# Keys turned on VectorE from the fourth batch on, queries turned eight slots sooner, and zeroing moved, in pooled attention followed by a mixture of experts

## The chip, the cores and the metric

The kernel runs on one core of a Trainium2 chip. The core has TensorE (PE, matrix products into PSUM), VectorE (DVE), ScalarE (ACT), GpSimd (POOL, which here issues the loads) and SyncE (SP, which issues the first loads and all output stores). The metric is the time on the device of one execution, in microseconds (us); lower is better. The kernel before takes 555.17 us, the median of three runs (555.05 to 555.86).

## The reference

The inputs are `q`, `k`, `v` of shape 8 batches x 8 heads x 576 tokens x 64, and the weights of four experts. Keys and values are averaged over groups of 8 tokens, which leaves 72 of each, every query attends to these 72, and the result goes through all four experts, weighted by given probabilities:

```python
k_p = k.reshape(B, H, Sp, pool, D).mean(axis=3)      # Sp = 72, pool = 8
v_p = v.reshape(B, H, Sp, pool, D).mean(axis=3)
scores = scale * np.matmul(q, k_p.transpose(0, 1, 3, 2))
scores = scores - np.max(scores, axis=-1, keepdims=True)
attn = np.exp(scores)
attn = attn / (np.sum(attn, axis=-1, keepdims=True) + 1e-09)
return np.matmul(attn, v_p)
...
# x: 4608 tokens x 512 (all heads of a token side by side)
for e in range(E):                                   # 4 experts, 512 -> 1024 -> 512
    h = np.maximum(x @ w1[e], 0.0)
    out += p[:, e:e + 1] * (h @ w2[e])
```

## The kernel before, in words

The 4608 tokens are 36 tiles of 128 tokens (t = 0 to 35); four tiles are a group, for which the experts are run with 512 columns. A step is one expert on one group, so there are 36 steps. Each step has 12 slots: in slots 0 and 1 of every three the up projection of the next step is issued, one block of 128 hidden units per slot (`up`, L655, eight matmuls of 512 columns; ScalarE then applies the ReLU, L659), in the third the down projection of one tile of this step (`down`, L687, eight matmuls of 512 columns), which VectorE weights and adds up (`collect`, L698 and L702). The sums leave through SP. The up and down projections fill TensorE; attention for later tiles is fitted between them.

What is fitted where is written out by hand. `at(slot, function, arguments)` puts a call into a dictionary, and after the projection of a slot the calls of that slot are issued, in the order in which they were put there. Every engine works through its own instructions in the order of issue, so a slot fixes a place in each engine's queue and not a time; from slot 12 on a slot takes some 1.2 us of TensorE. Nothing is planned by a cost model.

`plan_tile(t, base, steps)` places attention for one tile. For tiles from DT = 9 on, `base` is 17 slots (tile 9: 14) before the slot in which the tile is due, thus 12 t - 65:

- `turn_q` (L454) at base: VectorE transposes the queries in blocks of 32 x 32 out of `qblk`, a buffer with one batch's queries (two buffers, loaded by `load_qblk`, L173, eight loads per batch of rows of 32 numbers). The result `qT` has four buffers.
- `scores` (L475) and `less_max` (L491, L498) at base + 2: TensorE multiplies `qT` by the turned keys `kT`, VectorE subtracts the row maximum.
- `expo` (L517, ScalarE) at base + 4; `normalise` (L541 to L544, VectorE) at base + 5: the row sums, their inverse, and the weights.
- `turn_e_part` (L571) at base + 6 to base + 9: VectorE turns the weights, 16 transposes of 32 partitions.
- `context_turned` (L629, TensorE, and L643, ScalarE) at base + 13: the products with the values.

Earlier tiles (t below 9) have their queries and weights turned by TensorE.

`plan_batch` places the work for one batch's keys and values, relative to the base of the first tile that needs that batch (from batch 3 on: tiles 13, 18, 22, 27 and 31, the batch edges). For keys: `fold_k` (L315) at base - 11 and base - 9 adds halves of the 8 pooled tokens, `end_k` (L325) at base - 8 does the last addition into `kpad`, `turn_k` at base - 5 turns it: five transposes on TensorE into PSUM (L344, `kT_ps`) and two copies by ScalarE (L353) into `kTh`, whose two halves (`y`) hold alternating heads with zeros between them. At end + 1, POOL loads the keys of the batch after next into the buffer that has become free (`load_k`, L107: `kraw`, two buffers). The values follow: folds at base - 1 and base, the last addition at base + 1 (L376), their spreading over blocks (L392) at base + 3, and the load of the batch after next at base + 2. The next batch's queries are loaded at base + 1, which waits until the buffer's last reader, `turn_q` of this tile, is done.

The prelude computes tiles 0 to 3 while expert weights arrive; it ends when the first weights of the second expert have landed. ScalarE zeroes several buffers at its beginning, and further ones after it: `vraw` (L903), then the mask `mask_h` (L286) in slot 1 and `kTh`, `eTh` and `vh` (L924) in slots 2 to 7. In the new kernel, KB = 3 is the first batch whose keys go the other way, WB = 2 is the one from which the halves `kTh` and `vh` are used, and BLK = 32, NW = 9, POOL = 8.

Of the kernel before, what the change touches and what calls it, by code (L numbers as in the profile page):

```python
# [12 lines left out]
BF16 = mybir.dt.bfloat16  # L13
# [4 lines left out]
def kernel(  # L18
# [10 lines left out]
    nc = tc.nc  # L29

    B, H, S, D = q.shape
    E, DM, F = moe_w1.shape
    P = nc.NUM_PARTITIONS
    POOL = 8
# [11 lines left out]
    NB = 5  # L46
    TAIL = ROWS - (NB - 1) * P
    DT = 2 * TPG + 1
    EXP_SCALE = 1.0 / (float(D) ** 0.5 * POOL)
    NZ = 4  # L50
    BLK = 32
# [3 lines left out]
    HR = ROWS // 2  # L55
    NW = HR // BLK

    SPAN = ((0, 0), (1, 0), (1, 1), (2, 1))
    assert H * D == DM and D == 64 and SP == 72 and P == 128 and TAIL == 64

# [4 lines left out]
    prep = ctx.enter_context(tc.tile_pool(name="prep", bufs=2))  # L65
# [15 lines left out]
    kraw = [raw.tile([P, NB, POOL * D], BF16, name=f"kraw{i}") for i in range(2)]  # L81
    vraw = [raw.tile([P, NB + 1, POOL * D], BF16, name=f"vraw{i}") for i in range(2)]
    ehalf, eTh, kTh = [], [], []
    vh = [raw.tile([P, len(SPAN), 2, 2, D], BF16, name=f"vh{i}") for i in range(2)]
    ebuf = [raw.tile([P, NB * P], BF16, name=f"ebuf{i}") for i in range(2)]
# [11 lines left out]
    def rows_of(src):  # L97
        return src.rearrange("h (j r) d -> (h j) (r d)", r=POOL)

    def load_rows(eng, dst, rows, parts=((0, NB - 1), (NB - 1, NB))):  # L100
        for i0, i1 in parts:
            if i1 == NB:
                src, to = rows[i0 * P:ROWS], dst[0:TAIL, i0, :]
            else:
                src = rows[i0 * P:i1 * P].rearrange("(i p) x -> p i x", p=P)
                to = dst[:, i0:i1, :]
            eng.dma_start(out=to, in_=src)  # L107

    def load_k(b):
        load_rows(nc.gpsimd, kraw[b % 2], rows_of(k[b]))  # L110

    def load_v(b):
        if b < WB:
# [85 lines left out]
    for c0 in range(0, TPG, 2):  # L199
        nc.sync.dma_start(  # L200
            out=qg[:, :, c0:c0 + 2, :],
            in_=q[0][:, 0:G, :].rearrange("h (p c) d -> p h c d", c=TPG)[
                :, :, c0:c0 + 2, :
            ],
# [16 lines left out]
    for sign, base in ((1, PW), (-1, -SP - 1)):  # L221
        nc.gpsimd.affine_select(
            out=own[:], in_=own[:], compare_op=ALU.is_ge, fill=0.0,
            base=base, channel_multiplier=sign,
# [5 lines left out]
    for sign, base in ((1, 0), (-1, SP - 1)):  # L230
        nc.gpsimd.affine_select(
            out=ownh[:], in_=ownh[:], compare_op=ALU.is_ge, fill=0.0,
            base=base, channel_multiplier=sign,
# [12 lines left out]
    load_w1(1)  # L246
    halves = (slice(0, FB // 2), slice(FB // 2, FB))
    load_k(1)
    load_q(TPG)
    load_w1(2, (0,))  # L250
# [25 lines left out]
    mask_v = const.tile([P, NB, MZ, D], BF16, name="mask_v")  # L276
    mask_h = const.tile([P, len(SPAN), 2, D], BF16, name="mask_h")

    def spread_mask():
        nc.scalar.copy(  # L280
            out=mask_v[:], in_=own[:, :, 1:NZ].unsqueeze(3).to_broadcast([P, NB, MZ, D])
        )

    def spread_mask_h():
        for n, (c, g) in enumerate(SPAN):
            nc.scalar.copy(  # L286
                out=mask_h[:, n], in_=ownh[:, c, g].unsqueeze(2).to_broadcast([P, 2, D])
            )
# [21 lines left out]
    kT, vblk, pads = {}, {}, {}  # L310

    def fold(rows, i0, i1, *widths):
        for n in widths:
            w = n * D
            nc.vector.tensor_add(  # L315
                out=rows[:, i0:i1, 0:w], in0=rows[:, i0:i1, 0:w],
                in1=rows[:, i0:i1, w:2 * w],
            )

    def last_k(b, rows, i0, i1, n=P):  # L320

        if b not in pads:
            pads[b] = prep.tile([P, NB, 2, D], BF16, name="kpad")
        shape = [n, i1 - i0, 2, D]
        nc.vector.tensor_add(  # L325
            out=pads[b][0:n, i0:i1],
            in0=rows[0:n, i0:i1, 0:D].unsqueeze(2).to_broadcast(shape),
            in1=rows[0:n, i0:i1, D:2 * D].unsqueeze(2).to_broadcast(shape),
        )

    def fold_k(b, n):
        fold(kraw[b % 2], 0, NB, n)

    def end_k(b):
        last_k(b, kraw[b % 2], 0, NB)

    def turn_k(b, odd=None, order=range(NB), between={}):

# [47 lines left out]
    def spread_v(b):  # L386
        if b >= WB:
            vblk[b] = vh[b % 2]
            for n, (c, g) in enumerate(SPAN):

# [231 lines left out]
    def context_turned(t):  # L622
        ps = ps_t.tile([P, KC, P], F32, tag="t", name="xT_ps")
        for b, _, n, at in segments(t * P, P):
            if t >= DT:
                for pair in range(NPAIR):
                    g, y = divmod(pair, 2)
                    for m in (2 * g, 2 * g + 1):
                        nc.tensor.matmul(  # L629
                            ps[:, pair, at:at + n],  # L630
                            lhsT=vblk[b][:, m, y].rearrange("p z d -> p (z d)"),
                            rhs=eT[t][:, SPAN[m][0], at:at + n, y],
                            start=(m == 2 * g), stop=(m == 2 * g + 1),
# [99 lines left out]
    SLOTS = 12  # L733
    plan = {}

    def at(slot, fn, *args):
        plan.setdefault(slot, []).append((fn, args))

    def plan_batch(b, fold4, fold2, end, turn, v_fold4, v_fold2, v_end, spread):
        at(fold4, fold_k, b, 4)  # L740
        at(fold2, fold_k, b, 2)
        at(end, end_k, b)
        at(turn, turn_k, b)
        if WB <= b < WB + 2:
            at(v_fold4 - 8, clear_v, b)
        at(v_fold4, fold_v, b, 4)
        at(v_fold2, fold_v, b, 2)
        at(v_end, end_v, b)
        at(spread, spread_v, b)
        if b + 2 < B:  # L750
            at(end + 1, load_k, b + 2)
            at(v_end + 1, load_v, b + 2)

    def plan_tile(t, base, steps):
        at(base, turn_q, t)
        at(base + steps[0], scores, t)
        at(base + steps[0], less_max, t)
        at(base + steps[1], expo, t)
        at(base + steps[2], normalise, t)
        if t < DT:  # L760
            at(base + steps[3], turn_e, t)
        else:
            for a in range(P // BLK):
                at(base + steps[3] + a, turn_e_part, t, a)
        at(base + steps[4], context_turned, t)
        return base + steps[4] + 1

    at(SLOTS - 4, domain_probs, dp1, TPG, DT)
    at(5 * SLOTS + 6, load_probs)
    at(7 * SLOTS + 5, domain_probs, dpr, DT, NT)  # L770
    plan_batch(1, 3, 4, 5, 7, 18, 19, 20, 21)
    for t in range(TPG, 2 * TPG):
        assert plan_tile(t, 12 + 3 * (t - TPG), (3, 5, 6, 9, 11)) <= 3 * SLOTS - 2
# [3 lines left out]
    for t in range(2 * TPG, NT):  # L777
        due = (t - TPG) * SLOTS
        if t < DT:
            lead, steps = 14, (2, 4, 5, 8, 10)  # L780
        else:

            lead, steps = 14 if t == DT else 17, (2, 4, 5, 6, 13)
        base = due - lead
        b = ((t + 1) * P - 1) // S
        if b > last_b:
            times = (-11, -9, -8, -5, -1, 0, 1, 3)
            if t == DT:
                times = (-6, -5, -4, -2, 2, 3, 4, 5)
            plan_batch(b, *(base + x for x in times))  # L790
            if 2 < b < B - 1:
                at(base + 1, load_qblk, b + 1)
            last_b = b
        assert plan_tile(t, base, steps) <= due - (0 if t == DT else 3)
# [3 lines left out]
    def warm(n):  # L798

        ps = ps_o.tile([P, 2 * P], F32, tag="o", name="warm_ps")  # L800
        for _ in range(n):
            nc.tensor.matmul(ps[:], lhsT=zero[:, 0:P], rhs=zero[:])

    act, dve = nc.scalar.copy, nc.vector.tensor_copy
    spread_mask()
    warm(22)
    fold(k0[0:TAIL], NB - 1, NB, 4, 2)
    last_k(0, k0, NB - 1, NB, TAIL)
# [81 lines left out]
    for i in range(2):  # L890
        for to, n, form in (
# [4 lines left out]
            part = room[:, at0:at0 + n]  # L896
            to.append(part.rearrange(form.pop("pattern"), **form))
            at0 += n
    zeros = [x for i in range(2) for x in (
        kTh[i][:], eTh[i][:, 2], vh[i][:, 1::2, :, 0]  # L900
    )]
    for t in vraw:
        nc.scalar.memzero(t[:, NB, :])  # L903
    at(1, spread_mask_h)
    for i, x in enumerate(zeros):
        at(2 + i, nc.scalar.memzero, x)
    load_k(2)
    load_qblk(2)
    load_v(2)
    load_qblk(3)  # L910

    for s in range(NSTEP):
        for slot in range(SLOTS):
            part, i = slot % 3, slot // 3
# [41 lines left out]
```

## Time and profile before

| | |
|---|---|
| median of three runs | 555.17 us (555.05 to 555.86) |
| the profiled execution | 555.2 us |
| its span, first to last instruction | 553.5 us |
| mean clock granted to TensorE | 0.999 of full speed |
| busy: TensorE, VectorE, ScalarE, POOL | 544.3, 384.9, 240.7, 81.7 us |
| up and down projections on TensorE (L655, L687) | 270.4 and 269.6 us |
| TensorE's waits that the profile lists | 5.4 us, 3.2 of them before the end of the prelude at 37.24 us |
| key transposes L344 on TensorE | 40, of 219 ns each, overlapping |

A line of the profile names the engine, the line of the kernel, the operation, the output and the inputs, the shapes and how many there are. In the order of time a line begins with its start and its length in us; what stands in brackets is the idle time of the engine ahead of it and what ended it. Matmuls overlap, so their lengths add up to more than the time that passes. Idle time of an engine that is not on the path that sets the end costs nothing.

### The profile page before, as it was taken

What the parts mean: (1) busy time and instruction counts of PE and PEld (TensorE: products, weight loads), DVE (VectorE), ACT (ScalarE), POOL (GpSimd) and SP (SyncE); (2) the same over time, 40 slices, a digit from 0 to 9 for tenths busy, and PEclk for the clock granted to TensorE, in tenths of its full rate; (3) what the DMA queues carried; (4) which work ended last, traced back from release to release, by engine and by line L of the source; (5) the groups of instructions that cost most, each with busy time, mean ns of one, the idle gap of its engine ahead of it and who ended that gap; (6) DMA issues with size and microseconds to landing.
All of it is one profiled execution on the core that took longest, in us unless ns stands there. A gap on an engine that the chain in (4) does not pass through costs nothing.

```text
span 553.5 us, 8005 instructions
## 1 busy us (share of the span) xinstructions
PE 544.3 (98%) x3110; PEld 270.6 (49%) x3110; DVE 384.9 (70%) x925; ACT 240.7 (43%) x422; POOL 81.7 (15%) x122
## 2 busy tenths in 40 slices
PE   7999999899999999999999999999999999999997
PEld 5854545444444444444444444444444444444444
DVE  5636946878977779877897778977897777622223
ACT  6764654344444444444444434444443444433330
POOL 6253381100240005100060004000000000000000
PEclk9999999999999999999999999999999999999999
DMA  9999999210590009900491019001000100001002
GB/s 226 207 200 206 182 110 197 43 6 0 101 103 2 1 38 108 60 1 19 101 60 27 2 76 44 1 1 58 19 2 0 53 25 1 2 38 39 0 1 76
DMA packets 88038, 33.69 MB, mean 61 GB/s; under 512 B 62656, under 2 KB 82944, under 8 KB 88000
## 3 DMA queue, kind: packets, MB, share of 16 engines
q0 software_dynamic: 75920, 21.44, 44.0%
q1 hardware_dynamic: 12080, 11.74, 6.3%
q8 instruction: 24, 0.39, 0.3%
q14 instruction: 14, 0.11, 0.1%
HBM read 45.16 MB, written 9.44 MB: 99 GB/s over the span
## 4 chain that ended last, share of the span: by engine, by line
PE 89%; DMA 5%; DVE 3%; POOL 1%; issue 0%; SPq 0%; DVEq 0%
PE o_ps L687 42%; PE h_ps L655 42%; DMA w<-in_moe_w_dram 5%; PE xT_ps L629 2%; PE sc L475 2%; DMA k<-in_k_dram 1%; DVE late L571 1%; POOL w L182 0%; DVE total L541 0%; PE kT_ps L344 0%; PE xT_ps L638 0%; PE last_ps L720 0%; DVE d_sb L498 0%; DVE ebuf L551 0%; DVE acc L698 0%
## 5 line engine op out<-in xcount | busy, mean ns | idle before, releaser
L655 PE MATMUL h_ps<-xT,w 128*128 128x512 bf16 x1120 | 270.4, 379 | 0.4 <-DMA w<-in_moe_w_dram 0.3
L687 PE MATMUL o_ps<-w,h_sb 128*128 128x512 bf16 x1144 | 269.6, 379 | 0.0
L659 ACT ACTIVATE h_sb<-h_ps 128x512 bf16<-128x512 f32 x280 | 167.1, 597 | 222.3 <-PE h_ps L655 221.6
L687 PEld LDWEIGHTS <-h_sb 128*128 128x128 bf16 x1144 | 111.9, 98 | 134.2
L655 PEld LDWEIGHTS <-w 128*128 128x128 bf16 x1120 | 106.3, 98 | 115.5 <-issue 1.0
L702 DVE SCALAR_TENSOR_TENSOR acc<-o_ps,p_sb,acc 128x512 f32<-128x512 f32 x107 | 80.2, 749 | 94.9 <-PE o_ps L687 93.6
L571 DVE STREAM_TRANSPOSE late<-late 32x64 f32<-32x64 f32 (+1 forms) x432 | 105.6, 244 | 6.9
L698 DVE TENSOR_SCALAR acc<-o_ps,p_sb 128x512 f32<-128x512 f32 x36 | 26.9, 747 | 34.9 <-PE o_ps L687 34.5
L173 POOL DMA_DIRECT2D qblk<-in_q_dram x48 | 38.9, 820 | 79.6 <-DVE qT L454 65.8
L643 ACT CAST xT<-xT_ps 128x512 bf16<-128x512 f32 x32 | 18.8, 586 | 49.5 <-PE xT_ps L629 42.9
L491 DVE TENSOR_REDUCE mx<-sc 128x8 f32<-128x576 f32 x34 | 25.7, 756 | 14.8 <-PE sc L475 14.4
L107 POOL DMA_DIRECT2D kraw<-in_k_dram x14 | 9.3, 667 | 146.6 <-DVE kpad L325 140.9
L498 DVE TENSOR_TENSOR d_sb<-sc,mx 128x576 f32<-128x576 f32 x34 | 25.7, 757 | 1.2
L541 DVE TENSOR_REDUCE total<-e_sb 128x8 f32<-128x576 f32 x32 | 23.8, 745 | 1.2 <-ACT e_sb L517 0.9
L544 DVE TENSOR_TENSOR late<-e_sb,rs 128x576 bf16<-128x576 f32 x27 | 21.7, 805 | 1.0
L517 ACT ACTIVATE e_sb<-d_sb 128x576 f32<-128x576 f32 x27 | 18.4, 683 | 5.0 <-DVE d_sb L498 4.7
L454 DVE STREAM_TRANSPOSE qT<-qblk 128x512 bf16<-128x512 bf16 (+1 forms) x30 | 19.1, 646 | 0.0
L629 PEld LDWEIGHTS <-vh 128*128 128x128 bf16 x240 | 14.8, 96 | 6.4
L475 PEld LDWEIGHTS <-qT 128*128 128x128 bf16 (+1 forms) x160 | 11.3, 100 | 11.4 <-DVE qT L454 2.8
L629 PE MATMUL xT_ps<-late,vh 128*128 128x128 bf16 (+1 forms) x240 | 16.8, 213 | 0.0
L124 POOL DMA_DIRECT2D vraw<-in_v_dram x24 | 14.5, 619 | 13.4 <-DVE v_half L376 12.4
L475 PE MATMUL sc<-late,qT 128*128 128x144 bf16 (+1 forms) x120 | 11.6, 227 | 1.8 <-DVE qT L454 1.8
(94 smaller groups left out, 201.8 us busy)
## 6 DMA issues: line engine op xcount, KB each, us to landing
out_dram<-acc SPq DMA_DIRECT2D x35, 256.0 KB, 2.0
w<-in_moe_w_dram POOLq DMA_DIRECT2D x12, 512.0 KB, 13.8
kraw<-in_k_dram POOLq DMA_DIRECT2D x7, 512.0 KB, 7.1
qblk<-in_q_dram POOLq DMA_DIRECT2D x48, 72.0 KB, 4.8
w<-in_moe_w_dram POOLq DMA_DIRECT2D x2, 1024.0 KB, 18.0
vraw<-in_v_dram POOLq DMA_DIRECT2D x6, 256.0 KB, 5.6
vraw<-in_v_dram POOLq DMA_DIRECT2D x6, 224.0 KB, 5.6
k<-in_k_dram SPq DMA_DIRECT2D x2, 512.0 KB, 4.5
```

Source lines behind the costliest of these rows:

```text
L173: nc.gpsimd.dma_start(out=to[:, g], in_=q[b][head:head + 2, :, half * BLK:(half + 1) * BLK] .rearrange("z (a i) d -> i (z a) d", i=BLK),)
L475: nc.tensor.matmul(banks[pair // 2][at:at + n, (pair % 2) * PW:(pair % 2 + 1) * PW], lhsT=qT[t][:, pair, at:at + n], rhs=kT[b][:, pair * P ...
L491: nc.vector.reduce_max(out=mx[:], in_=view, axis=AX.X)
L498: nc.vector.tensor_tensor(out=ds[t][:, g], in0=view, in1=mx[:].unsqueeze(3).to_broadcast([P, n, 4, SP]), op=ALU.subtract,)
L541: nc.vector.reduce_sum(out=total[:], in_=e, axis=AX.X)
L571: nc.vector.transpose(out=dst.rearrange("p (c k) -> p c k", k=P)[:, 0:n, toks], in_=src.rearrange("p (c k) -> p c k", k=P)[:, 0:n, rows],)
L629: nc.tensor.matmul(ps[:, pair, at:at + n], lhsT=vblk[b][:, m, y].rearrange("p z d -> p (z d)"), rhs=eT[t][:, SPAN[m][0], at:at + n, y], st ...
L655: nc.tensor.matmul(ps[:], lhsT=w1_sb[e][:, kc, fb * P:(fb + 1) * P], rhs=xT[g][:, kc, :], start=(kc == 0), stop=(kc == KC - 1),)
L659: nc.scalar.activation(out=hs[s][:, fb, :], in_=ps[:], func=ACT.Relu)
L687: nc.tensor.matmul(ps[:], lhsT=hs[s][:, fb, i * P:(i + 1) * P], rhs=w2_sb[e][:, fb, :], start=(fb == 0), stop=(fb == FB - 1),)
L698: nc.vector.tensor_scalar_mul(out=accs[t][:], in0=ps[:], scalar1=p_sb[:, e, t:t + 1])
L702: nc.vector.scalar_tensor_tensor(out=accs[t][:], in0=ps[:], scalar=p_sb[:, e, t:t + 1], in1=accs[t][:], op0=ALU.mult, op1=ALU.add,)
```

## The change

It has four parts.

1. From batch 3 on, keys are loaded in another layout: each partition holds 32 of the 64 numbers of 72 tokens of one head. A batch takes eight loads, each of 16 partitions x 72 rows of 32 numbers (128 bytes as f32), in place of two loads of whole rows of eight tokens (2 KB).
2. For these batches the folds and the last addition work on that layout (1152, 576 and 288 elements a partition, before 1280, 640 and 640), and VectorE turns the keys by two transposes of 64 partitions x 288 elements, one at base - 5 and one at base - 4, straight into `kTh`. The five transposes on TensorE and the two copies on ScalarE go. The transposes write each run of 32 keys nine elements apart.
3. The queries of tiles 10 to 35 are turned at base - 8, not at base. On VectorE's queue that moves them ahead of `normalise` and `turn_e_part` of the tile before, at a batch edge ahead of the turning of the keys and the folds of the values, and for tile 10 ahead of `less_max` of tile 9 and all that follows.
4. The zeroing of `vraw` and `vh` and the spreading of `mask_h` move to the beginning of the kernel, behind the first mask; that of `kTh` and `eTh` moves from slots 2 to 6 to slots 14, 17, 20 and 23.

```diff
+    KB = 3
...
+    def k_blocks(b):
+
+        return kraw[b % 2][:].rearrange("p i x -> p (i x)")[
+            :, 0:NW * POOL * BLK
+        ].rearrange("p (a x) -> p a x", x=POOL * BLK)
+
     def load_k(b):
-        load_rows(nc.gpsimd, kraw[b % 2], rows_of(k[b]))
+        if b < KB:
+            load_rows(nc.gpsimd, kraw[b % 2], rows_of(k[b]))
+            return
+
+        for n32 in range(P // BLK):
+            y, half = divmod(n32, 2)
+            for g in range(2):
+                head, p0 = 4 * g + 2 * y, n32 * BLK + g * BLK // 2
+                nc.gpsimd.dma_start(
+                    out=k_blocks(b)[p0:p0 + BLK // 2].rearrange(
+                        "i a (r d) -> i (a r) d", d=BLK
+                    ),
+                    in_=k[b][head:head + 2, :, half * BLK:(half + 1) * BLK].rearrange(
+                        "z (i n) d -> (z i) n d", n=NW * POOL
+                    ),
+                )
...
     def fold_k(b, n):
-        fold(kraw[b % 2], 0, NB, n)
+        if b < KB:
+            fold(kraw[b % 2], 0, NB, n)
+            return
+        w = n * BLK
+        rows = k_blocks(b)
+        nc.vector.tensor_add(
+            out=rows[:, :, 0:w], in0=rows[:, :, 0:w], in1=rows[:, :, w:2 * w]
+        )
 
     def end_k(b):
-        last_k(b, kraw[b % 2], 0, NB)
+        if b < KB:
+            last_k(b, kraw[b % 2], 0, NB)
+            return
+        pads[b] = prep.tile([P, NW, BLK], BF16, name="khalf")
+        rows = k_blocks(b)
+        nc.vector.tensor_add(
+            out=pads[b][:], in0=rows[:, :, 0:BLK], in1=rows[:, :, BLK:2 * BLK]
+        )
+
+    def turn_k_by_blocks(b, y):
+        half = slice(y * D, (y + 1) * D)
+        kT[b] = kTh[b % 2]
+        nc.vector.transpose(
+            out=kT[b][half, y].rearrange("d (i a) -> d a i", a=NW), in_=pads[b][half],
+        )
...
-        at(turn, turn_k, b)
+        if b < KB:
+            at(turn, turn_k, b)
+        else:
+            for y in range(2):
+                at(turn + y, turn_k_by_blocks, b, y)
...
-        at(base, turn_q, t)
+        at(base - (8 if t > DT else 0), turn_q, t)
...
     spread_mask()
+    for i in range(2):
+        nc.scalar.memzero(vraw[i][:, NB, :])
+        nc.scalar.memzero(vh[i][:, 1::2, :, 0])
+    spread_mask_h()
...
-    zeros = [x for i in range(2) for x in (
-        kTh[i][:], eTh[i][:, 2], vh[i][:, 1::2, :, 0]
-    )]
-    for t in vraw:
-        nc.scalar.memzero(t[:, NB, :])
-    at(1, spread_mask_h)
+    zeros = [x for i in range(2) for x in (kTh[i][:], eTh[i][:, 2])]
     for i, x in enumerate(zeros):
-        at(2 + i, nc.scalar.memzero, x)
+        at(SLOTS + 3 * i + 2, nc.scalar.memzero, x)
```

## The prediction

> **What bounds the kernel now.** I read the page's engine totals first, then the list of waits of TensorE, then the order of time around each wait, and last the groups for durations.
>
> ```profile
> PE 544.3 (98%) x3110; PEld 270.6 (49%) x3110; DVE 384.9 (70%) x925; ACT 240.7 (43%) x422; POOL 81.7 (15%) x122
> ```
>
> TensorE (PE) is busy 98% of the span, so an edit counts where it takes work off TensorE or ends a wait of TensorE. Its waits, all of them:
>
> ```profile
> PE sc L475 <- DVE qT L454: 1.8, 1, 1.8
> PE kT_ps L344 <- DVE kpad L325: 1.4, 2, 1.0
> PE warm_ps L802 <- DVE zero L215: 1.1, 1, 1.1
> PE sum_ps L585 <- DVE rs L535: 0.4, 1, 0.4
> PE sc L475 <- DVE d_sb L498: 0.4, 1, 0.4
> PE h_ps L655 <- DMA w<-in_moe_w_dram: 0.3, 1, 0.3
> ```
>
> The columns are total us, times, longest us. Only the first lies in the main loop behind 66 us. In order of time, TensorE and then VectorE (DVE) around it, and an ordinary batch edge:
>
> ```profile
> 101.95 1.03 PE L655 MATMUL h_ps<-xT,w 128*128 128x512 bf16 x4
> 104.78 0.42 PE L475 MATMUL sc<-late,qT 128*128 128x144 bf16 x4 [1.80 <-DVE qT L454]
> ...
> 107.63 0.62 PE L629 MATMUL xT_ps<-late,vh 128*128 128x128 bf16 x8
> ```
> ```profile
> 92.21 0.94 DVE L315 TENSOR_TENSOR vraw<-vraw 128x1536 bf16<-128x1536 bf16 x1
> ...
> 95.25 0.75 DVE L698 TENSOR_SCALAR acc<-o_ps,p_sb 128x512 f32<-128x512 f32 x1 [0.16 <-PE o_ps L687]
> ...
> 100.91 3.08 DVE L571 STREAM_TRANSPOSE late<-late 32x96 f32<-32x96 f32 x12
> 104.01 0.71 DVE L454 STREAM_TRANSPOSE qT<-qblk 128x512 bf16<-128x512 bf16 x1
> ```
> ```profile
> 140.59 0.44 PE L344 MATMUL kT_ps<-ident,kpad 128*128 128x128 bf16 x5
> 140.86 1.46 PE L655 MATMUL h_ps<-xT,w 128*128 128x512 bf16 x6
> ```
> ```profile
> 211.52 0.48 DVE L325 TENSOR_TENSOR kpad<-kraw 128x640 bf16<-128x640 bf16 x1
> 211.92 0.75 DVE L541 TENSOR_REDUCE total<-e_sb 128x8 f32<-128x576 f32 x1
> ...
> 216.00 3.08 DVE L571 STREAM_TRANSPOSE late<-late 32x96 f32<-32x96 f32 x12
> ```
>
> The scores of tile 10 wait for its queries, which VectorE turns only behind everything it owes tile 9 (104.01, behind the last turned weights at 103.99). The reader is also to see that a matmul group's printed length overlaps the next one: five key transposes last 0.44 us, but the next group starts 0.28 us after them (140.59 to 140.86). Starts, not lengths, give what TensorE saves.
>
> **The change part by part.** All sums are against the profiled execution, 555.2 us, a span of 553.5 and 1.7 around it; the median shown is 555.17, so the two may be taken as one.
>
> *Keys off TensorE, batches 3 to 7.* Removed: 5 x 5 transposes. By starts, five take 0.27 to 0.28 us, in all 1.4 us of TensorE; the printed 0.44 us would make it 2.2, and I keep that as the far end. Ten ScalarE copies (L353, 0.393 us each) go too; ScalarE is busy 43% and TensorE never waits for them, so they count as nothing. Gain: 1.4 us.
>
> *Keys onto VectorE.* Per batch two transposes of 64 partitions x 288 elements of bf16. The query transposes of L454 take 702 ns for 512 elements and 420 for 256, 1.10 ns an element, so 288 give 0.455 us. But they write their elements 9 apart (18 bytes), which no transpose of the trace does. Two rows bound it: L544 writes bf16 two apart at 805 ns against 757 of L551 for the same 576 elements (0.08 ns an element more, 0.48 us here); L295 writes f32 144 bytes apart, 108 elements in 347 ns, where the line through L498 (757 ns for 576, 448 for 288, so 1.07 ns an element) gives 255, thus 0.85 ns an element more, 0.70 us here. I take 0.48, as the row with the same type and the nearer step. [...] As worked out below, the sum is the same by 0.48 and by 0.70. The folds shrink: 1280, 640 and 640 elements at 815, 483 and 485 ns become 1152, 576 and 288, by the line through L315 and L376 (815 at 1280, 345 at 384: 0.525 ns an element) 0.75, 0.45 and 0.29 us, 0.3 us less, 0.19 of it behind the last idle VectorE has there.
>
> *Queries 8 slots sooner, tiles 10 to 35.* For tile 10 the turn goes from behind the weights of tile 9 to ahead of the value fold of 92.21. TensorE starts the matmuls before the wait at 101.95; four of their kind take 0.86 us elsewhere, so the scores could start at 102.82 and not at 104.78: 1.96 us gained (the listed 1.80 leaves out the overlap). Who pays: everything of tile 9 on VectorE, by 0.63 us (104.01 to 104.64) less the 0.16 idle of 95.25. Its weights end at 104.46, and their user, the context product of 107.63, comes at 105.67: 1.2 us are left. At tile 13 the scores start at 149.25, the four matmuls before them at 148.23: another 0.16 us. For the other tiles TensorE does not wait for queries, so nothing is gained; the turn of 0.70 us now stands ahead of the row sums of the tile before and delays its weights by up to 0.70 us, where on ordinary tiles 2.5 us are free (weights end at 203.98, context at 206.49). The wait of the query loads for the buffer (65.8 us of POOL, three times) ends sooner, so those loads move up some 9 us; their data is needed 50 us later.
>
> *Both together at a batch edge.* This is the tight place. At 211 to 221 us VectorE has no idle time, the weights of tile 17 end at 219.08, and the context product starts at 221.29: 2.21 us of room. TensorE arrives 0.28 sooner, leaving 1.93. New ahead of those weights: 0.70 for the queries of tile 18, less 0.19, plus two key turns. At 0.48 each that is 1.47, with 0.46 to spare; at 0.70 each 1.91, and just enough. **From 0.71 us a turn, TensorE waits at all five edges**, for twice the excess each (the other edges have 2.2 to 2.4 us). Sum: nothing, by bounds of 0 and of the rivals below. What follows the weights on VectorE, the value folds and the collection of a product (221.86), comes some 0.7 us later; two PSUM buffers for the products leave over 3 us.
>
> *Loading.* Keys from batch 3: eight loads of 128-byte rows, not two of 2 KB rows. The like of them is L173: 0.81 us of POOL each, so 6.5 us for 1.3, five times. Queued behind them on POOL are the values of the next batch (80.97, now from 86.2; folded at 147), queries and values (149.49; the keys' loads of 138.78 end by 145.4). Cover: keys of batch 3 are issued at 79.67 and folded at 134, later ones a batch ahead, over 45 us. If that cover were gone, each us late would be a us of TensorE. SP's output stores share the engines, but no engine waits for them before the end. I take 0.
>
> *Zeroing.* Seven kinds of ScalarE work move. Masks and zeros for values (0.7 + 0.6 + 0.9 us at L903, L924, L286) go ahead of the first key copy, where ScalarE idles 3.31 us before 9.09; at most 2.2 fit. Were it 1 us late there, the prelude still ends with the expert weights' load at 37.24. The four others (0.44, 0.30 twice) go to slots 14 to 23 (45 to 62 us), into idle stretches of 1 to 2 us of ScalarE; the hidden activations behind them have 1.8 us until their buffer is wanted. Gain at the old place: at most the 0.3 us load wait, which is not theirs. I take 0.
>
> Sum: 1.4 + 1.96 + 0.16 = 3.5 us; 555.2 - 3.5 = **551.7 us**.
>
> **The rivals.**
> *Some of it returns at the edges.* Key turns of 0.71 to 0.94 us: at 0.85 the wait is 5 x 2 x 0.14 = 1.4 us, 553.1. For it: a new write pattern, with L295 at the limit. Against: only L295 is that dear, and its step is eight times as long.
> *Key turns make it slower.* From 0.71 + 3.5/10 = 1.06 us a turn the gain is gone, from 1.17 the kernel is over 0.2% slower; at 1.3, 5 x 2 x 0.59 = 5.9 us, 557.6. For it: VectorE has no idle time there, and every excess lands on TensorE. Against: it needs 2.1 ns an element more than L454's, two and a half times L295's surcharge. [...]
> *Tile 10's wait only moves.* The context product of tile 9 waits in place of the scores, because VectorE is full from 92 to 107 us: the 1.96 is lost, 553.6. Against: the 1.2 us worked out.
> *The small-row loads are late* and stop TensorE: at 5 us an edge, 575. Against: 45 us of cover, and query loads of the same rows that no engine of the main loop waits for.
>
> **How the numbers follow.** A measurement here tells some 0.2% (1.1 us) from no change. The forecast has 0.66, with its own range of 550.9 (2.2 for the transposes) to 552.4. Part returned at the edges 0.09 (552.4 to 554.0), the wait that moves 0.06 (553 to 554); these are faster too, 0.81 together. Within 0.2%, by turns of 0.94 to 1.17 us, 0.05. Slower 0.14: the dear turns 0.11, late loads 0.03. The range runs from 550.9 to 554.6; it leaves out the slower cases and most of the unchanged.
>
> **What would show it.** No wait of scores for queries at 103 us; ten key transposes on VectorE of about 0.48 us and no kT_ps after batch 2; no wait of the context product (L629) for the turned weights (L571). Key turns over 0.71 us with such waits would make me wrong; so would a fold of keys that waits for its load.

## The result, and the profile after

The changed kernel takes 557.55 us (median of five, 557.46 to 557.98) against 555.05 us (554.80 to 555.86): a ratio of 1.0045, 95% interval 1.0031 to 1.0060. It is slower by 2.5 us; the prediction was 3.5 us faster, with a range up to 554.6. The profiled execution took 557.54 us, a span of 555.8. (One correction to the text ahead of the prediction: an up projection is four matmuls of 512 columns, not eight.)

The engine totals of the page of after, in the form shown before:

```profile
PE 539.2 (97%) x3030; PEld 268.8 (48%) x3085; DVE 397.0 (71%) x935; ACT 236.7 (43%) x412; POOL 106.5 (19%) x152
```

TensorE has less work and the kernel is longer, so TensorE waits. The two largest entries of its list of waits in after (total us, times, longest us), and among the costliest groups of after the new transposes of keys (busy us, mean ns of one, idle before):

```profile
PE xT_ps L673 <- DVE late L615: 6.4, 5, 1.5
PE kT_ps L388 <- DVE kpad L348: 1.5, 2, 1.1
```
```profile
L377 DVE STREAM_TRANSPOSE late<-khalf 64x288 bf16<-64x288 bf16 x10 | 14.5, 1445 | 0.1
```

The wait of the scores for the queries is gone; a wait of the context product (L673, before L629) for the turned weights (L615, before L571) has come, once at each of the five batch edges. A key turn takes 1.445 us, where 0.48 was forecast. The edge of the fourth window of the prediction, VectorE and then TensorE in order of time:

```profile
212.27 1.02 DVE L615 STREAM_TRANSPOSE late<-late 32x96 f32<-32x96 f32 x4
213.32 0.75 DVE L742 TENSOR_SCALAR acc<-o_ps,p_sb 128x512 f32<-128x512 f32 x1
214.10 1.02 DVE L615 STREAM_TRANSPOSE late<-late 32x96 f32<-32x96 f32 x4
215.13 1.45 DVE L377 STREAM_TRANSPOSE late<-khalf 64x288 bf16<-64x288 bf16 x1
216.60 1.02 DVE L615 STREAM_TRANSPOSE late<-late 32x96 f32<-32x96 f32 x4
217.63 1.44 DVE L377 STREAM_TRANSPOSE late<-khalf 64x288 bf16<-64x288 bf16 x1
219.09 1.03 DVE L615 STREAM_TRANSPOSE late<-late 32x96 f32<-32x96 f32 x4
```
```profile
217.17 1.89 PE L731 MATMUL o_ps<-w,h_sb 128*128 128x512 bf16 x8
220.16 0.62 PE L673 MATMUL xT_ps<-late,vh 128*128 128x128 bf16 x8 [1.10 <-DVE late L615]
```

The two turns stand between the parts of the weights, VectorE has no gap, and the product starts as the last part ends (220.12). Eight matmuls of a down projection take 1.73 us from start to start, so the product could have started at 218.90: 1.26 us lost, 0.16 more than the 1.10 listed, as at tile 10 in the kernel before.

The account from the two traces: the five waits cost 6.4 + 5 x 0.16 = 7.2 us. Against them stand 1.96 and 0.16 us of scores that no longer wait, 1.4 of key transposes, 0.7 at the end of the prelude (below), and 0.4 by which TensorE reached the up projections sooner in this execution (32.61 us for 33.04), whose first load also landed sooner (3.60 us for 4.07; in the traces of the other kernels it takes 3.6 to 4.5). That the load is the reason is likely, not shown. 7.2 - 4.6 = 2.6 us, where the spans differ by 2.3.

### The profile page after: what moved, and what is told of

It reads as the page before. It is cut to its first block, busy times and chain, and to the rows that moved or that the text cites. A ratio compares the mean times of both kernels' runs of the same rounds, so it can differ in the third digit from the quotient of the medians.

```text
span 555.8 us, 7927 instructions
## 1 busy us (share of the span) xinstructions
PE 539.2 (97%) x3030; PEld 268.8 (48%) x3085; DVE 397.0 (71%) x935; ACT 236.7 (43%) x412; POOL 106.5 (19%) x152
## 3 DMA queue, kind: packets, MB, share of 16 engines
q0 software_dynamic: 119600, 21.44, 84.6%
## 4 chain that ended last, share of the span: by engine, by line
PE 84%; DVE 12%; issue 2%; DMA 1%; DVEq 0%; SPq 0%; ACT 0%; ACTq 0%
PE o_ps L731 39%; PE h_ps L699 38%; DVE late L615 3%; PE xT_ps L673 2%; DVE late L377 2%; PE sc L519 2%; PE h_ps L714 1%; DVE total L585 1%; DVE late L588 1%; DVE acc L746 1%; DVE d_sb L542 1%; DMA k<-in_k_dram 1%; DVE qT L498 1%; DVE mx L535 1%; DVE k L338 0%
## 5 line engine op out<-in xcount | busy, mean ns | idle before, releaser
L699 PE MATMUL h_ps<-xT,w 128*128 128x512 bf16 x1088 | 267.6, 379 | 2.0
L731 PE MATMUL o_ps<-w,h_sb 128*128 128x512 bf16 x1121 | 266.7, 379 | 0.9
L703 ACT ACTIVATE h_sb<-h_ps 128x512 bf16<-128x512 f32 x280 | 167.0, 597 | 224.1 <-PE h_ps L699 223.2
L615 DVE STREAM_TRANSPOSE late<-late 32x64 f32<-32x64 f32 (+1 forms) x432 | 105.6, 244 | 7.0
L126 POOL DMA_DIRECT2D kraw<-in_k_dram x40 | 31.4, 795 | 135.3 <-DVE khalf L370 132.9
L673 PE MATMUL xT_ps<-late,vh 128*128 128x128 bf16 (+1 forms) x240 | 16.8, 213 | 6.4 <-DVE late L615 6.4
L673 PEld LDWEIGHTS <-vh 128*128 128x128 bf16 x240 | 14.8, 96 | 13.6 <-issue 7.8
L377 DVE STREAM_TRANSPOSE late<-khalf 64x288 bf16<-64x288 bf16 x10 | 14.5, 1445 | 0.1
```

The source lines that it names most:

```text
L126: nc.gpsimd.dma_start(out=k_blocks(b)[p0:p0 + BLK // 2].rearrange("i a (r d) -> i (a r) d", d=BLK), in_=k[b][head:head + 2, :, half * BLK: ...
L615: nc.vector.transpose(out=dst.rearrange("p (c k) -> p c k", k=P)[:, 0:n, toks], in_=src.rearrange("p (c k) -> p c k", k=P)[:, 0:n, rows],)
L673: nc.tensor.matmul(ps[:, pair, at:at + n], lhsT=vblk[b][:, m, y].rearrange("p z d -> p (z d)"), rhs=eT[t][:, SPAN[m][0], at:at + n, y], st ...
L699: nc.tensor.matmul(ps[:], lhsT=w1_sb[e][:, kc, fb * P:(fb + 1) * P], rhs=xT[g][:, kc, :], start=(kc == 0), stop=(kc == KC - 1),)
L703: nc.scalar.activation(out=hs[s][:, fb, :], in_=ps[:], func=ACT.Relu)
L731: nc.tensor.matmul(ps[:], lhsT=hs[s][:, fb, i * P:(i + 1) * P], rhs=w2_sb[e][:, fb, :], start=(fb == 0), stop=(fb == FB - 1),)
```

## The experiments

Three questions: is it the step of the written elements that makes a turn dear; what does each part of the change give by itself; and is the room at a batch edge what the prediction said. The diffs are against the changed kernel; under "The parts alone" those of the queries and of the zeroing are against the kernel before.

### Turns that write in a row

```diff
-            out=kT[b][half, y].rearrange("d (i a) -> d a i", a=NW), in_=pads[b][half],
+            out=kT[b][half, y].rearrange("d (a i) -> d a i", a=NW), in_=pads[b][half],
```

> The changed kernel, but the two key turns of a batch write their 32 keys in a row and not nine elements apart. This puts the keys of a head into another order in kT, so the scores belong to other keys; amount of work, loads and waits stay. Theory 1 (the write nine elements apart is the price of 1.445 us a turn): a turn takes 0.46 us as by the query turns, no wait of the context product for the turned weights at the batch edges, 555.1 - 1.96 - 0.16 - 1.4 - 0.7 = 550.9 us. Rival (64 partitions or 2-byte blocks of 32 x 9 are the price, not the step of the write): turns stay at 1.4 us and the time at 557.5 us.

Measured: 550.62 us (550.30 to 550.93), ratio 0.9910 (0.9894 to 0.9925). Its group of key turns, and all waits of its TensorE:

```profile
L377 DVE STREAM_TRANSPOSE late<-khalf 64x288 bf16<-64x288 bf16 x10 | 4.7, 473 | 0.1
```
```profile
PE warm_ps L850 <- DVE zero L238: 1.1, 1, 1.1
PE kT_ps L388 <- DVE kpad L348: 1.0, 2, 0.6
PE sc L519 <- DVE d_sb L542: 0.4, 1, 0.4
PE sum_ps L629 <- DVE rs L579: 0.4, 1, 0.4
```

Same partitions, same number of elements, same loads: the places that are written alone make the difference between 0.47 and 1.45 us a turn, and with the dear write go all five waits and 6.9 us. Theory 1 holds.

### What a step costs

The comments in this diff are added here.

```diff
+        s3 = src[:, 0:288].rearrange("p (a i) -> p a i", i=32)      # 64 partitions
...
+        tr(out=far(1), in_=s3)      # L969: transposes of bf16, step 1
+        tr(out=far(2), in_=s3)      # L970 to L977: steps 2, 3, 4, 6, 8, 9, 16, 32
...
+        cp(out=far(1), in_=s3)      # L978 to L983: copies, steps 1, 2, 4, 8, 9, 16
...
+        tr(out=farf(1), in_=f3)     # L992 to L994: transposes of f32, steps 1, 2, 9
...
+    at(SLOTS * 33 + 2, probe_writes)
```

> The changed kernel with 18 extra instructions of VectorE near the end, where VectorE idles and the buffers are free: transposes and plain copies of 64 partitions x 288 elements, with steps of the written elements of 1 to 32 elements of bf16, and transposes of f32 with steps of 1, 2 and 9. [...] Theory 1b (any step over one element makes a transpose dear, at once): 0.46 us at a step of 1, 1.4 us from 2 on, copies stay under 0.7 us, as the line that writes f32 144 bytes apart. Rival (64 partitions): 1.4 us at a step of 1 too.

Measured: 570.35 us in one execution, which says nothing by itself, since the 18 instructions hold VectorE while a product waits to be collected (8.7 us of TensorE's waits). Some of the probes among its groups (transposes of bf16 with steps of 8, 9, 3 and 1 at L974, L975, L971 and L969, copies with 9 and 8 at L982 and L981, f32 with 9 and 2 at L994 and L993):

```profile
L974 DVE STREAM_TRANSPOSE kraw<-vraw 64x288 bf16<-64x288 bf16 x1 | 1.5, 1453 | 0.0
L975 DVE STREAM_TRANSPOSE kraw<-vraw 64x288 bf16<-64x288 bf16 x1 | 1.4, 1440 | 0.0
...
L982 DVE COPY kraw<-vraw 64x288 bf16<-64x288 bf16 x1 | 1.4, 1400 | 0.0
...
L981 DVE COPY kraw<-vraw 64x288 bf16<-64x288 bf16 x1 | 0.8, 795 | 0.0
L994 DVE STREAM_TRANSPOSE kraw<-vraw 64x288 f32<-64x288 f32 x1 | 0.7, 685 | 0.0
...
L971 DVE STREAM_TRANSPOSE kraw<-vraw 64x288 bf16<-64x288 bf16 x1 | 0.7, 654 | 0.0
...
L993 DVE STREAM_TRANSPOSE kraw<-vraw 64x288 f32<-64x288 f32 x1 | 0.5, 471 | 0.0
...
L969 DVE STREAM_TRANSPOSE kraw<-vraw 64x288 bf16<-64x288 bf16 x1 | 0.5, 461 | 0.0
```

All of them, in ns:

| step in elements | 1 | 2 | 3 | 4 | 6 | 8 | 9 | 16 | 32 |
|---|---|---|---|---|---|---|---|---|---|
| transpose, bf16 | 461 | 494 | 654 | 814 | 1131 | 1453 | 1440 | 1389 | 1418 |
| copy, bf16 | 226 | 321 | | 479 | | 795 | 1400 | 1348 | |
| transpose, f32 | 470 | 471 | | | | | 685 | | |

A transpose of bf16 is cheap up to a step of two (461 and 494 ns), rises by some 0.16 us for each further element, and is flat from eight elements on (1389 to 1453 ns). A plain copy nine apart takes 1.40 us too, so the price is not the transpose's alone. And f32 pays far less: nine apart, 0.685 us, thus 0.75 ns an element more than in a row, where bf16 pays 3.4 ns. Theory 1b does not hold: a step of two costs a transpose 33 ns more than writing in a row. Nor does the rival: in a row, 64 partitions take 461 ns. Copies grow with the step too, but at eight they are not yet at their top (795 ns, and 1400 at nine); and no step of f32 between two and nine was run. The probe also changes one thing besides the step: up to eight it writes the nine runs of 32 one behind another, from nine on each between the others, as the changed kernel does. For transposes this makes no difference that shows (1453 ns at eight, 1440 at nine), so there the step is the price; for copies the two cannot be told apart. What makes the cost of transposes flat from eight elements on is not shown, and why bf16 pays more than f32 stays open, as does why a copy eight apart is at 0.80 us and the transpose at 1.45.

### The order put right: by the loads, or by TensorE's reads

Blocks of 32 successive keys on 32 partitions let the turn write in a row and in order. Each block takes a load of its own, or two.

```diff
-            out=kT[b][half, y].rearrange("d (i a) -> d a i", a=NW), in_=pads[b][half],
+            out=kT[b][half, y].rearrange("d (a i) -> d a i", a=NW), in_=pads[b][half],
...
+                f0 = 0
+                while f0 < 2 * SP:
+                    a0, i0 = divmod(g * 2 * SP + f0, BLK)
+                    n = min(BLK - i0, 2 * SP - f0)
+                    nc.gpsimd.dma_start(
+                        out=rows[i0:i0 + n, a0],
+                        in_=src[f0 * POOL:(f0 + n) * POOL].rearrange(
+                            "(i r) d -> i r d", r=POOL
+                        ),
+                    )
+                    f0 += n
```

> The changed kernel, but the keys are loaded so that a block of 32 partitions holds 32 successive pooled keys; the turn then writes in a row and the keys are in order. That takes 40 loads a batch of up to 32 partitions x 8 rows of 128 bytes, in place of 8. Theory 1: turns of 0.46 us and, if 40 loads of some 0.6 us of POOL (24 us a batch, with 60 us between batches) stay hidden, 550.9 us. Rival: the loads of queries and values queued behind them come late, folds wait for them, and the time is above 553 us.

Measured: 551.00 us (550.74 to 551.51), ratio 0.9915 (0.9896 to 0.9934). The 40 loads hold POOL for 22.3 us a batch, and no engine of the main loop waits for what is queued behind them. The same kernel once more, beside the one with runs of three keys that follows:

> The kernel with the keys loaded so that 32 successive pooled keys fill a block of 32 partitions (40 loads a batch), once more on the same chip as the one with runs of three: 551.0 us as before, and within 0.3 us of it by theory.

Measured: 550.29 us (550.13 to 551.05), ratio 0.9902 (0.9886 to 0.9919). That is 0.5 us under the kernel with runs of three (550.82), where 0.3 was expected; the runs of each spread by more, 0.9 and 2.3 us.

The other way leaves the loads of the change and lets TensorE read apart:

```diff
-                    else kT[b][:, :, pair * SP:(pair + 1) * SP],
+                    else kT[b][:, :, pair * SP:(pair + 1) * SP] if b < KB
+                    else kT[b].rearrange("p y (a c i) -> p y c i a", a=NW, c=NPAIR)[
+                        :, :, pair
+                    ],
```

> The changed kernel, but the turn writes in a row and TensorE reads the turned keys 32 elements apart in the scores of batches 3 to 7, which puts them in order. Theory 1: turns of 0.46 us; if TensorE reads with this step at the price of a row, 550.9 us. Rival: the step costs TensorE what it costs VectorE, three times as much again for some 100 matmuls of 0.064 us each, 18 us more, 569 us.

Measured: 568.91 us (566.85 to 569.18, three executions; a fourth took 1486.15 us, for which nothing here gives a reason, and is left out), ratio 1.0228 (1.0200 to 1.0256): near the rival's 569. One group of scores with TensorE's work on both sides, in this kernel and in that with turns in a row:

```profile
223.49 1.02 PE L702 MATMUL h_ps<-xT,w 128*128 128x512 bf16 x4
224.35 1.14 PE L519 MATMUL sc<-late,qT 128*128 128x144 bf16 x4
225.32 1.04 PE L702 MATMUL h_ps<-xT,w 128*128 128x512 bf16 x4
```
```profile
217.67 1.02 PE L699 MATMUL h_ps<-xT,w 128*128 128x512 bf16 x4
218.53 0.41 PE L519 MATMUL sc<-late,qT 128*128 128x144 bf16 x4
218.78 1.03 PE L699 MATMUL h_ps<-xT,w 128*128 128x512 bf16 x4
```

From start to start four matmuls take 0.97 us, not 0.25: 0.24 us each in place of 0.06. The traces hold 20 such groups of four for batches 3 to 7 (0.71 us more each) and three groups at tiles that span two batches (1.09 us for 0.39), 16.3 us in all. The two spans differ by 18.9 us, but 2.0 of that is lost before 28 us, ahead of all these scores, in an execution whose granted clock was 0.94 there (1.00 in the other). So the step costs some 16.3 to 16.9 us; that the time met the rival's 569 so closely is in part chance. TensorE too pays for a read of bf16 32 elements apart.

### Runs of three keys: the room at the edge

```diff
+            for g, f0, i0, n in ((0, 0, 0, 32), (1, 96, 0, 16), (1, 0, 16, 16), (2, 48, 0, 32)):
...
+                        "(i r) d -> i r d", r=3 * POOL
...
-            out=kT[b][half, y].rearrange("d (i a) -> d a i", a=NW), in_=pads[b][half],
+            out=kT[b][half, y].rearrange("d (g i c) -> d g c i", g=3, c=3),
+            in_=pads[b][half].rearrange("p (g c) x -> p g c x", g=3),
```

> The changed kernel with its keys loaded in runs of three: a partition holds three successive pooled keys in each of three groups of 96, so the turn writes three elements apart (6 bytes) and the keys are in order; 16 loads a batch of up to 32 partitions x 24 rows of 128 bytes. By the probe, a transpose that writes three apart takes 0.654 us. Theory (at a batch edge VectorE has room for two turns of 0.65 to 0.7 us before TensorE waits, as predicted from the trace of before; only the price was wrong): no wait of the context product for the turned weights, 550.6 to 551.2 us. Rival (any dearer turn lands on TensorE at once, the room is not there): 5 x 2 x 0.19 = 1.9 us more than with turns in a row, 552.5 us or more.

Measured: 550.82 us (550.42 to 552.67), ratio 0.9917 (0.9897 to 0.9937). The same edge, VectorE and TensorE:

```profile
214.19 0.66 DVE L381 STREAM_TRANSPOSE late<-khalf 64x288 bf16<-64x288 bf16 x1
...
215.89 0.66 DVE L381 STREAM_TRANSPOSE late<-khalf 64x288 bf16<-64x288 bf16 x1
216.56 1.03 DVE L620 STREAM_TRANSPOSE late<-late 32x96 f32<-32x96 f32 x4
```
```profile
216.08 1.89 PE L736 MATMUL o_ps<-w,h_sb 128*128 128x512 bf16 x8
217.81 0.62 PE L678 MATMUL xT_ps<-late,vh 128*128 128x128 bf16 x8
```

The weights end at 217.59, the product starts 1.73 us after the projection before it and waits for nothing. With turns of 0.655 us 0.2 us are left here (0.2 to 0.4 at the five edges), so TensorE would wait from about 0.76 us a turn; 0.71 was worked out from the trace of before. The room was sized right.

### The parts alone

Queries alone:

```diff
-        at(base, turn_q, t)
+        at(base - (8 if t > DT else 0), turn_q, t)
```

> The kernel before with queries turned 8 slots sooner from tile 10 on, and nothing else. Theory: the wait of the scores of tile 10 (1.96 us) and that of tile 13 (0.16) go, 555.1 - 2.1 = 553.0 us. Rival: the wait moves to the context product of tile 9, 554.5 to 555.1 us.

Measured: 552.66 us (552.54 to 553.12), ratio 0.9958 (0.9946 to 0.9970): 2.4 us by the medians. The scores of tile 10 start 0.87 us after the matmuls before them, and the context product of tile 9 does not wait.

Zeroing alone:

```diff
     spread_mask()
+    for i in range(2):
+        nc.scalar.memzero(vraw[i][:, NB, :])
+        nc.scalar.memzero(vh[i][:, 1::2, :, 0])
+    spread_mask_h()
...
-        at(2 + i, nc.scalar.memzero, x)
+        at(SLOTS + 3 * i + 2, nc.scalar.memzero, x)
```

> The kernel before with the zeroing moved, and nothing else. Theory (the trace of after: four up projections at 33 us follow one another in 3.46 us, where before they took 4.18 because their ReLUs stood behind zeroing on ScalarE): 554.4 us, and no gap of TensorE ahead of 37 us. Rival (as predicted, nothing): 555.1 us.

Measured: 554.30 us against 555.07, ratio 0.9990 (0.9981 to 0.9998), which is a gain of 0.1 to 1.1 us; the size is better read from the trace. TensorE and ScalarE in the kernel before, and TensorE with the zeroing moved:

```profile
33.04 3.83 PE L655 MATMUL h_ps<-xT,w 128*128 128x512 bf16 x16
37.22 1.89 PE L655 MATMUL h_ps<-xT,w 128*128 128x512 bf16 x8 [0.35 <-DMA w<-in_moe_w_dram]
```
```profile
35.46 0.88 ACT L286 COPY mask_h<-ownh 128x128 bf16<-128x128 bf16 x4
36.25 0.44 ACT L924 ACTIVATE late<-late 128x288 uint32<-128x288 uint32 x1
36.59 0.58 ACT L659 ACTIVATE h_sb<-h_ps 128x512 bf16<-128x512 f32 x1
```
```profile
32.83 5.34 PE L655 MATMUL h_ps<-xT,w 128*128 128x512 bf16 x23
38.01 0.44 PE L344 MATMUL kT_ps<-ident,kpad 128*128 128x128 bf16 x5
```

Before, 16 matmuls take 4.18 us from start to start; with the zeroing away, 24 (one is missing from the trace) take 5.18, or 3.45 for 16. The 0.7 us were lost to ReLUs that stood behind zeroing on ScalarE and held the two buffers of the up projection. The profile of before puts the gap down to a load of weights; that of the kernel with the keys alone (the last of this section), which zeroes at the old place, puts the same 0.35 us down to the ReLU (L703).

Both together, without the keys, the last two diffs:

> The change without its keys: queries sooner and zeroing moved. Theory: the two gains add, 555.1 - 2.1 - 0.7 = 552.3 us, thus 5.2 us faster than the whole change. Rival (the parts share a gain): 553.0 us or more.

Measured: 552.42 us (551.63 to 554.84), ratio 0.9955 (0.9937 to 0.9973). The runs spread too far to tell 552.3 from 553.0 by time. The trace has neither gap. Its prelude reaches the up projections 0.8 us later than that of before (33.80 against 33.04), for a reason that stays open, and its span is 2.3 us shorter all the same.

Keys alone, with queries and zeroing as before:

```diff
-        at(base - (8 if t > DT else 0), turn_q, t)
+        at(base, turn_q, t)
...
-        at(SLOTS + 3 * i + 2, nc.scalar.memzero, x)
+        at(2 + i, nc.scalar.memzero, x)
```

> The kernel before with the keys of the change alone: loads, folds and turns on VectorE; queries and zeroing as before. Theory (VectorE's queue at a batch edge is full, so every us ahead of the turned weights lands on TensorE): the weights end 2.73 us later where 1.93 are free, 0.8 us of wait; the queries, turned behind the value folds, come 2.73 us later too and make the scores wait 1.5 us more; 555.1 - 1.4 + 5 x 2.3 = 565 us. Rival (the parts only add): 557.55 + 2.1 + 0.7 = 560.4 us.

Measured: 567.13 us (565.74 to 567.87), ratio 1.0213 (1.0197 to 1.0228). TensorE's waits, and the edge on TensorE:

```profile
PE sc L519 <- DVE qT L498: 9.1, 6, 2.2
PE xT_ps L673 <- DVE late L615: 3.1, 5, 0.7
```
```profile
225.07 0.62 PE L673 MATMUL xT_ps<-late,vh 128*128 128x128 bf16 x8 [0.70 <-DVE late L615]
225.53 1.02 PE L699 MATMUL h_ps<-xT,w 128*128 128x512 bf16 x3
227.94 0.42 PE L519 MATMUL sc<-late,qT 128*128 128x144 bf16 x4 [1.38 <-DVE qT L498]
```

Two waits, at this edge 0.86 and 1.54 us with the 0.16 each that the list leaves out, where 0.8 and 1.5 were expected. The median is 2.1 us above the expected 565. Some of that is seen in the trace: the scores wait 2.17 us at the first edge, and 0.4 us are lost before it. The rest is not accounted for. The parts do not add: the queries turned sooner are worth 2.4 us without the keys and some 9 with them (567.13 less 557.55, less 0.7 for the zeroing), because they leave VectorE's queue before the dear turns enter it.

## Why the prediction was wrong

- **The step that failed is the price of a key turn**, "I take 0.48, as the row with the same type and the nearer step", and its far end, 0.70. It measured 1.445 us. The row with the same type (L544) has a step of two, which the probe shows to be nearly free for a transpose (494 ns against 461); the row with the far step (L295) is f32, which pays 0.75 ns an element in the probe and bf16 3.4. Each row had one of the two things that matter, none had both, and I took the pair for bounds. The ends were no bounds: a 2-byte write nine apart was not in the trace.
- The mechanism stood in the text: "From 0.71 us a turn, TensorE waits at all five edges". By that formula 1.445 us give 5 x 2 x 0.735 = 7.4 us; the trace has 7.2. The sign that it gave for being wrong, key turns over 0.71 us with waits of the context product, is what the trace shows. The rival that key turns make it slower, 557.6 us at 1.3, had 0.11 and was the one that came. That its 557.6 meets the 557.55 measured is chance: at 1.445 us a turn its formula gives 559.1, and what the forecast left out, the 0.7 of the zeroing above all, lies between. The reason given against it, that it needs two and a half times L295's surcharge, did not hold: the surcharge is 3.4 ns an element, four times L295's.
- Right: 1.96 and 0.16 us of scores (2.4 measured alone), 1.4 of key transposes (not measured alone, but the account needs it), the folds (0.75, 0.45 and 0.30 us), the room of the edge, and the loads. The packets of the software queue took 84.6% of the engines' span in after, 44.0% before, and no fold of batches 3 to 7 waited for a key.
- Wrong and small: zeroing, "I take 0". It gave 0.7 us, because I took the 0.3 us that the list of waits puts down to a load at its word, and did not compare the starts of matmuls there as I did at tile 10. And 575 for late loads should be 576.7 by its own terms (551.7 and 25); nothing rests on it.
- With a turn of 0.47 and the zeroing, the sum is 555.2 - 3.5 - 0.7 = 551.0: the kernel with turns in a row took 550.62.

## What to carry to other kernels

Before a layout puts a strided write on an engine whose queue is full, look for a row with the same element size and at least that step; if there is none, the price is open, and a probe of a dozen instructions where the engine idles settles it. Here the stride could go into the loads: 40 small loads a batch cost nothing that the times show (551.00 and 550.29 us, against 550.62 with eight and the keys out of order), nor did 16 with runs of three keys (550.82), while the step cost VectorE 1 us a turn or TensorE 0.18 us a matmul. Where a queue is full, sizing the room in us ahead of the next consumer gives the threshold, and moving another instruction out of that queue can be worth several times what it is worth alone, as the queries were here: some 9 us with the dear turns, 2.4 without.

## What the hardware showed that was not expected

VectorE writes bf16 nine elements apart at 1.40 to 1.45 us for 64 x 288 elements, copies as transposes, against 0.23 and 0.46 in a row; f32 with the same number of elements between takes 0.685. For transposes of bf16 the cost is flat from a step of eight elements on (1453 ns at eight, 1389 to 1440 beyond). TensorE reading bf16 32 elements apart takes 0.24 us for 144 columns, against 0.06. The version that beats both kernels is the change with its keys loaded so that the turn writes in a row: 551.00 and 550.29 us, or 550.82 with 16 loads a batch.
